# Delta-rule attention and feed-forward network on one core: the order of the work ahead of the first block's output rewritten

## The chip, the cores and the metric

The kernel runs on one core of a Trainium2 chip. The core has five engines that run at the same time, each with its own list of instructions in order: TensorE (PE; its weight loads are listed apart as PEld), VectorE (DVE), ScalarE (ACT), GpSimd (POOL) and SyncE (SP), which issues most of the transfers (DMA). They wait for each other by semaphores. The metric is the device time of one execution in microseconds (us); lower is better.

## What is computed

For each of 4 batches and 8 heads a state of 48 x 48 is carried over 768 steps, and what the state gives for each query goes through a feed-forward network with 2048 inner columns.

```python
k_n = k / (np.linalg.norm(k, axis=-1, keepdims=True) + 1e-06)
for t in range(S):
    y[:, :, t] = np.einsum('bhd,bhde->bhe', q[:, :, t], state)
    v_old = np.einsum('bhde,bhd->bhe', state, kt)
    state = state + bt[:, :, :, None] * np.einsum('bhd,bhe->bhde', kt, vt - v_old)
h = x @ w_in
g = np.where(h >= 1, h, np.where(h <= -1, 0.0, (h + 1) ** 2 / 4))
out = g @ w_out
```

Here x is y with its heads laid side by side, 3072 tokens of 384.

## The kernel before

The 768 steps are cut into 12 blocks g of 64 steps, and blocks are taken in pairs G of two. Within a block the recurrence becomes matrix products. `gram_k` makes the keys' products (64 x 64 for each head) and `gram_q` those of queries with keys; the latter have to be masked to the steps ahead of the query. For a pair, `lanes` lays the key products out, takes the norms (a square root on ACT, then small DVE instructions) and scales them; `solve` inverts triangles of 16 x 16 in 15 steps of two DVE instructions each (lines L355 and L357); `unlanes` writes the result back. `merge16_a`, `merge16_b` and two halves of `merge32` grow the inverse to 64 x 64, with TensorE products and an eviction after each. Then `chain_u` makes the block's updates (its eviction: DVE copies at L514 into the tile SZ and L517 into SU, ACT copies at L517), `chain_y` the outputs (L539 and L541 for the first block; high part by ACT at L556, low part by DVE at L561), `chain_d` adds to the state.

The feed-forward weights come as 16 tiles `wt0` to `wt15` (768 KB each, packed). Each tile is unpacked by `grow` (ACT, L189), `shift` and `join` (DVE, L195 and L201), `cast` (ACT, L205) and `low` (DVE, L208). The network goes through 16 column tiles f for every pair ("items"; the first pair takes some tiles half by half): `up` (L738) makes h on TensorE, ACT and DVE make g out of it (L877, L891, L893, then L856 and L857 for the high and low part), and `down` (L753) accumulates the output two items later.

Two tables of code letters set the order by hand. `FRONT` has seven strings, one for each of the first block's seven chain pieces (merge16_a, merge16_b, two halves of merge32, chain_u, chain_y, chain_d); letters ahead of the comma are emitted between the piece's products and its eviction, letters behind it after the eviction. `FILL` has one string for each item. The letters: A and D the next unpacking step on ACT or DVE; F one dummy product of zeros on TensorE (L165, `dense`); L the next part of `lanes(1)`, the norms of the second pair; S one step of `solve(1)`; s and t the scaling of V for block 0 and 1 (L292); m and M the masking of the query products of block 0 and 1; w the load of the next weight tile; l the next load of keys, queries or values. Each engine runs what it gets in this order and waits at the first instruction that isn't ready.

SP issues loads in order, with eight transfers under way at most: each load waits for the one eight places ahead of it. PSUM banks come from a rotating list `START` (`acc`).

Of the kernel before, what the change touches and what calls it, by code (L numbers as in the profile page):

```python
# [7 lines left out]
F32 = mybir.dt.float32  # L8
# [5 lines left out]
C = 64  # L14
# [15 lines left out]
FRONT = (  # L30
    "sAwFALs,", "FLFFFDFFLFFFFF,F", "FFDD,S", "mFFFFFmm,", "AFFFD,AAw", ",", "DA,Dt")
FILL = (
# [8 lines left out]
def delta_rule_moe(ctx: ExitStack, tc: tile.TileContext, kqa, kqb, kv, beta, w, out):  # L41
# [20 lines left out]
    P = 128  # L62
# [8 lines left out]
    K, KE, GE, Q, KV, XB, RAW, WT = {}, {}, {}, {}, {}, {}, {}, {}  # L71
    START = [dict(name=n, bufs=b) for n, b in (("ch", 2), ("ch", 2), ("h", 2), ("h", 2), ("o2", 1), ("o3", 1), ("o0", 1))]
    spare = []
# [46 lines left out]

    def weight_loads(n0, n1, q=nc.sync):
        for f in range(n0, n1):
            RAW[f] = const.tile([P, 2, 2 * DM], F32, name=f"wt{f}")
            q.dma_start(out=RAW[f].bitcast(I32), in_=w.bitcast(I32)[:, f])

# [10 lines left out]
    load_kv(0)  # L136
    weight_loads(2, 5)
    load_kv(1)
# [27 lines left out]
    dense(WARM)  # L166
    mask = const.tile([P, C], F32, name="mask")
    nc.gpsimd.memset(mask, 1.0)
    for r in (0, C):
        nc.gpsimd.affine_select(out=mask[r:r + C], in_=mask[r:r + C], pattern=[[1, C]], base=0,  # L170
                                channel_multiplier=-1, compare_op=ALU.is_gt, fill=0.0)
    mid = const.tile([P, 1], F32, name="half")
# [71 lines left out]
    def gram_q(g):  # L244
# [12 lines left out]
        def evict():  # L257
            def raw():
                for a, b, r in moved():
                    nc.scalar.copy(out=a, in_=b)  # L260

            def masks(copied=False):
                for a, b, r in moved():
                    nc.vector.tensor_tensor(out=a, in0=a if copied else b, in1=mask[r, None, :].broadcast_to([r.stop - r.start, H, C]), op=ALU.mult)
                    yield

            def later():
                raw()
                for a, b, r in moved():
                    for c in range(r.start, r.stop, C):  # L270
                        y = x[c:c + C, 0 if r.stop - r.start > C else c // C, (0, H)[r.stop - r.start > C]:(H, NU)[r.stop - r.start > C]]
                        nc.gpsimd.affine_select(out=y, in_=y, pattern=[[0, H], [1, C]], base=0, channel_multiplier=-1,  # L272
                                                compare_op=ALU.is_gt, fill=0.0)
            return (raw, masks(True)) if g < 2 else lambda: run(masks()) if g < 4 else later()
        return evict
# [382 lines left out]

    spare += START
    acts = [(f, grow) for f in range(2)] + [x for f in range(FT) for x in ((f + 2, grow), (f, cast)) if x[0] < FT]  # L660
    vecs = [x for f in range(FT + 1) for x in ((f, shift), (f, join), (f - 1, low)) if 0 <= x[0] < FT]
    sv, ln, raws = [scale_v(g) for g in range(4)], [lanes(0), lanes(1)], []
    tasks = {"A": unpack(acts), "D": unpack(vecs), "B": restore(), "L": ln[1], "s": sv[0], "t": sv[1], "v": sv[2], "z": sv[3]}
    loads = [(load_k, 3), (load_q, 2), (load_kv, 2), (load_q, 3), (load_kv, 3), (load_k, 4)]
    tile_ = [5]

    def do(codes):
        for c in codes:
            if c in "wW":
                weight_loads(tile_[0], tile_[0] + 1, nc.scalar if c == "W" else nc.sync)  # L670
                tile_[0] += 1
# [32 lines left out]
    one_ = lambda f, *a: [lambda: f(*a)]  # L704
    place_beta(1, NS)()
    stage(one_(merge16_a, 0), 0)
    stage(one_(merge16_b, 0), 1)
    tasks.update({"m": raws[0][1], "M": raws[1][1], "S": solve(1), "U": unlanes(1)})
    stage(one_(merge32, 0, None, True), 2)
# [3 lines left out]
    stage(both(chain_d, 0), 6)  # L713
    spare[:] = START[0:2] + START[4:6]

# [234 lines left out]
```

## Time and profile before

| | before |
|---|---|
| median of 3 runs | 589.5 us (588.17 to 590.91) |
| profiled execution | 590.3 us, its span 588.6 us |
| TensorE busy | 569.0 us (97%) |
| VectorE busy | 405.2 us (69%) |
| ScalarE busy | 327.5 us (56%) |
| GpSimd busy | 54.5 us (9%) |
| TensorE clock granted, mean | 0.992 of full |

The span is the time between the first and the last instruction; 1.7 us of the profiled execution lie outside it. Busy time is shared out over 40 equal slices on the profile page; there, TensorE's first slices are less full than the rest, the granted clock is 7 tenths in the third slice (29.4 to 44.1 us) and full behind it, and VectorE is at 8 to 9 tenths from the fifth slice to the eighth and at 3 to 9 tenths after that. A dummy product counts as busy TensorE time.

### The profile page before, as it was taken

To read this page: it belongs to the slowest core of one execution; us is meant where nothing else is said; L and a number is where in the kernel's file an instruction comes from. 1 tells how busy PE (TensorE), PEld (TensorE's weight loads), DVE (VectorE), ACT (ScalarE), POOL (GpSimd) and SP (SyncE) were. 2 spreads that over 40 slices of the span, in tenths; PEclk is the share of its full clock that TensorE was granted. 3 is DMA by queue.
4 is the path that set the end of the run, shared out by engine and by line. 5 is a ranking of instruction groups with operands and counts; after the bars stand their busy time and mean duration, and the time that the engine had idled before them with its cause. 6 is when DMAs were issued, how large, how long until landed. Compare 5 with 4: busy or idle time off the path is not lost.

```text
span 588.6 us, 21697 instructions
## 1 busy us (share of the span) xinstructions
PE 569.0 (97%) x9585; PEld 493.3 (84%) x9585; DVE 405.2 (69%) x828; ACT 327.5 (56%) x587; POOL 54.5 (9%) x91
## 2 busy tenths in 40 slices
PE   8998899999999999999999999999999999999996
PEld 7776788788978888888888888888888888898986
DVE  5977999963689864599954599954599955333332
ACT  4648886358644575545575445575445564454443
POOL 6200010000000500010400011300011300000000
PEclk9979999999999999999999999999999999999999
DMA  5673766200333111134011134011133000020001
GB/s 147 199 253 138 213 212 192 77 4 10 95 81 100 31 32 39 39 97 114 24 33 41 37 103 119 16 30 45 36 106 96 1 3 16 15 55 1 0 2 53
DMA packets 32302, 42.77 MB, mean 73 GB/s; under 512 B 7056, under 2 KB 26768, under 8 KB 32208
## 3 DMA queue, kind: packets, MB, share of 16 engines
q1 hardware_dynamic: 31216, 40.41, 24.0%
q8 instruction: 75, 1.23, 0.9%
q0 software_dynamic: 576, 0.57, 0.4%
q10 hardware_dynamic: 416, 0.39, 0.2%
q14 instruction: 19, 0.16, 0.1%
HBM read 34.47 MB, written 4.72 MB: 67 GB/s over the span
## 4 chain that ended last, share of the span: by engine, by line
PE 47%; issue 22%; DVE 14%; DMA 6%; SPq 6%; ACT 2%; POOL 1%; POOLq 0%; DVEq 0%; ACTq 0%
PE h L738 18%; PE o L753 17%; DMA wt<-in_w_dram 4%; PE ch L534 3%; PE ch L237 2%; DVE s L893 2%; PE ch L508 2%; DVE pr L366 1%; DVE A L368 1%; DVE glo L857 1%; PE ch L250 1%; SPq L595 1%; PE ch L492 1%; DMA KV<-in_kv_dram 1%; DVE wt L208 1%
## 5 line engine op out<-in xcount | busy, mean ns | idle before, releaser
L738 PE MATMUL h<-xb,wt 128*128 128x512 f32 (+1 forms) x918 | 223.0, 386 | 5.1 <-DVE s L893 2.0
L753 PE MATMUL o<-wt,ghi 128*128 128x384 f32 x768 | 200.0, 342 | 0.1
L738 PEld LDWEIGHTS h<-xb,wt 128*128 128x128 f32 x918 | 161.8, 188 | 38.9 <-DVE s L893 3.4
L753 PEld LDWEIGHTS o<-wt,ghi 128*128 128x128 f32 x768 | 137.2, 188 | 7.0 <-issue 0.3
L753 PE MATMUL o<-wt,glo 128*128 128x384 f32 x384 | 129.4, 337 | 0.4 <-DVE glo L857 0.4
L856 ACT CAST ghi<-s 128x512 fp32r<-128x512 f32 (+1 forms) x102 | 60.8, 597 | 120.4 <-DVE s L893 107.8
L893 DVE SCALAR_TENSOR_TENSOR s<-s,h 128x512 f32<-128x512 f32 (+1 forms) x102 | 66.3, 650 | 77.1 <-ACT s L891 76.8
L877 ACT ACTIVATE s<-h,half 128x512 f32<-128x512 f32 (+1 forms) x102 | 67.4, 661 | 53.8 <-PE h L738 53.6
L857 DVE TENSOR_TENSOR glo<-s,ghi 128x512 fp32r<-128x512 f32 (+1 forms) x102 | 66.8, 654 | 39.5 <-ACT ghi L856 39.3
L753 PEld LDWEIGHTS o<-wt,glo 128*128 128x128 f32 x384 | 72.1, 188 | 1.0 <-DVE glo L857 1.0
L891 ACT ACTIVATE s<-s 128x512 f32<-128x512 f32 (+1 forms) x102 | 62.2, 610 | 2.2
L368 DVE TENSOR_TENSOR A<-A,pr 128x30 f32<-128x30 f32 (+14 forms) x120 | 45.4, 378 | 4.4
L366 DVE TENSOR_TENSOR pr<-A 128x30 f32<-128x30 f32 (+14 forms) x120 | 43.4, 362 | 2.2
L272 POOL TENSOR_SCALAR_AFFINE_SELECT Q<-Q 64x512 f32<-64x512 f32 x32 | 21.7, 680 | 117.4 <-ACT Q L260 116.0
L165 PE MATMUL o<-wx 128*128 128x512 f32 x87 | 27.8, 464 | 1.5 <-DVE tiny L175 1.5
L534 PEld LDWEIGHTS ch<-Q,SU 64*64 64x64 f32 (+3 forms) x1056 | 22.4, 135 | 3.7 <-ACT ghi L856 1.5
L534 PE MATMUL ch<-Q,SU 64*64 64x64 f32 (+3 forms) x1056 | 24.7, 222 | 0.0
L331 POOL TENSOR_SCALAR_AFFINE_SELECT A<-A 128x1024 f32<-128x1024 f32 x4 | 5.6, 1390 | 191.5 <-DMA xb<-X 148.1
L165 PEld LDWEIGHTS o<-wx 128*128 128x128 f32 x87 | 18.2, 220 | 5.6 <-DVE tiny L175 1.5
L626 DVE TENSOR_TENSOR SU<-ch,SU 48x384 f32<-48x384 f32 x36 | 19.9, 554 | 3.9 <-PE ch L607 3.5
L590 DVE TENSOR_TENSOR X<-ch,X 128x128 fp32r<-128x128 f32 x20 | 5.8, 292 | 23.5 <-ACT xb L586 22.5
L517 ACT COPY SU<-ch 64x384 f32<-64x384 f32 (+1 forms) x30 | 14.3, 476 | 7.0 <-PE ch L508 6.7
(168 smaller groups left out, 559.5 us busy)
## 6 DMA issues: line engine op xcount, KB each, us to landing
wt<-in_w_dram SPq DMA_DIRECT2D x16, 768.0 KB, 5.6
out_dram<-wx SPq DMA_DIRECT2D x44, 96.0 KB, 2.2
KV<-in_kv_dram SPq DMA_DIRECT2D x36, 96.0 KB, 2.4
KV<-in_kv_dram SPq DMA_DIRECT2D x72, 48.0 KB, 2.3
KV<-in_kv_dram SPq DMA_DIRECT2D x12, 192.0 KB, 2.7
xb<-X SPq DMA_DIRECT2D x60, 32.0 KB, 2.0
K<-in_kqb_dram SPq DMA_DIRECT2D x12, 128.0 KB, 2.6
Q<-in_kqb_dram SPq DMA_DIRECT2D x12, 128.0 KB, 2.7
```

Of the source, the lines that this page charges most:

```text
L165: nc.tensor.matmul(warm_ps, warm[:, 0:P], warm, start=True, stop=True)
L272: nc.gpsimd.affine_select(out=y, in_=y, pattern=[[0, H], [1, C]], base=0, channel_multiplier=-1, compare_op=ALU.is_gt, fill=0.0)
L366: nc.vector.tensor_tensor(out=pr, in0=A[:, 0:n, j:j + 1].broadcast_to([P, n, m]), in1=A[:, j:j + 1, j + 1:32].broadcast_to([P, n, m]), op= ...
L368: nc.vector.tensor_tensor(out=A[:, 0:n, j + 1:32], in0=A[:, 0:n, j + 1:32], in1=pr, op=ALU.add)
L534: nc.tensor.matmul(yy[i][o * C:o * C + C, e, p], SF[rows, u:u + C], w_[rows, x, k, :], **how)
L738: nc.tensor.matmul(h[:, cols(bs)], WT[f][:, 0, x, k * P:(k + 1) * P], XB[G][:, y, k, cols(bs)], start=(n == 0), stop=(n == 8))
L753: nc.tensor.matmul(oacc[G, k], (ghi, glo)[x][:, k * P:(k + 1) * P], WT[f][:, 1, y, :], start=(new and n == 0), stop=(left[G, b] == 0 and n ...
L856: nc.scalar.copy(out=ghi[:, c], in_=s[:, c])
L857: nc.vector.tensor_tensor(out=glo[:, c], in0=s[:, c], in1=ghi[:, c], op=ALU.subtract)
L877: nc.scalar.activation(out=s[:, c], in_=h[:, c], func=AF.Relu, bias=mid, scale=0.5)
L891: nc.scalar.activation(out=s[:, c], in_=s[:, c], func=AF.Square)
L893: nc.vector.scalar_tensor_tensor(out=s[:, c], in0=s[:, c], scalar=1.0, in1=h[:, c], op0=ALU.min, op1=ALU.max)
```

## The change

FRONT is rewritten; FILL is not touched. Ahead of the first block's output there are now 15 dummy products, where there were 23. The norms of the second pair (the last two L) and five solve steps (S) stand between the second half of merge32 and chain_u's eviction; before, the norms stood around merge16_b and one solve step behind the first half of merge32. All maskings of query products go to POOL (`select`, affine_select), where blocks 0 to 3 were masked by a DVE product with a mask tile; blocks 2 and 3 get an ACT copy out of PSUM ahead of it. Weight tiles 2 to 4 are no longer loaded between the values of block 0 and block 1: each of the tiles 2 to 6 is loaded by a w of FRONT, and a DVE memset of one element of its room holds its transfer until DVE gets there. For the first two tiles cast comes ahead of the grow of the tile two further on. The rotating list of banks is reordered.

```diff
 FRONT = (
-    "sAwFALs,", "FLFFFDFFLFFFFF,F", "FFDD,S", "mFFFFFmm,", "AFFFD,AAw", ",", "DA,Dt")
+    "sAFFFALs,", "FFFFmmmMMM,wD", "FFD,", "FFFw,LLSS", "AFFFSSS,AwD", "DDw,", "Aw,ASDt")
...
-    START = [dict(name=n, bufs=b) for n, b in (("ch", 2), ("ch", 2), ("h", 2), ("h", 2), ("o2", 1), ("o3", 1), ("o0", 1))]
+    START = [dict(name=n, bufs=b) for n, b in (("ch", 2), ("ch", 2), ("o2", 1), ("o3", 1), ("h", 2), ("h", 2), ("o0", 1))]
...
-    def weight_loads(n0, n1, q=nc.sync):
+    def weight_loads(n0, n1, q=nc.sync, gate=False):
         for f in range(n0, n1):
             RAW[f] = const.tile([P, 2, 2 * DM], F32, name=f"wt{f}")
+            if gate:
+                nc.vector.memset(RAW[f][0:1, 0, 0:1], 0.0)
             q.dma_start(out=RAW[f].bitcast(I32), in_=w.bitcast(I32)[:, f])
...
     load_kv(0)
-    weight_loads(2, 5)
     load_kv(1)
...
-    mask = const.tile([P, C], F32, name="mask")
-    nc.gpsimd.memset(mask, 1.0)
-    for r in (0, C):
-        nc.gpsimd.affine_select(out=mask[r:r + C], in_=mask[r:r + C], pattern=[[1, C]], base=0,
-                                channel_multiplier=-1, compare_op=ALU.is_gt, fill=0.0)
...
-            def masks(copied=False):
-                for a, b, r in moved():
-                    nc.vector.tensor_tensor(out=a, in0=a if copied else b, in1=mask[r, None, :].broadcast_to([r.stop - r.start, H, C]), op=ALU.mult)
-                    yield
-
-            def later():
-                raw()
+            def select():
                 for a, b, r in moved():
                     for c in range(r.start, r.stop, C):
                         y = x[c:c + C, 0 if r.stop - r.start > C else c // C, (0, H)[r.stop - r.start > C]:(H, NU)[r.stop - r.start > C]]
                         nc.gpsimd.affine_select(out=y, in_=y, pattern=[[0, H], [1, C]], base=0, channel_multiplier=-1,
                                                 compare_op=ALU.is_gt, fill=0.0)
-            return (raw, masks(True)) if g < 2 else lambda: run(masks()) if g < 4 else later()
+                    yield
+
+            def later():
+                raw()
+                run(select())
+            return (raw, select()) if g < 2 else later
...
-    acts = [(f, grow) for f in range(2)] + [x for f in range(FT) for x in ((f + 2, grow), (f, cast)) if x[0] < FT]
+    acts = [(f, grow) for f in range(2)] + [x for f in range(FT) for x in (((f + 2, grow), (f, cast)) if f > 1 else ((f, cast), (f + 2, grow))) if x[0] < FT]
...
-    tile_ = [5]
+    tile_ = [2]
...
-                weight_loads(tile_[0], tile_[0] + 1, nc.scalar if c == "W" else nc.sync)
+                weight_loads(tile_[0], tile_[0] + 1, gate=tile_[0] < 7)
...
-    spare[:] = START[0:2] + START[4:6]
+    spare[:] = START[0:4]
```

Line numbers in the rows below are those of the kernel before; the changed kernel's are 4 or 5 lower (L424 becomes L419).

On TensorE, at the first block's merges and chain_u, before (L405 is merge16_a, L419 merge16_b, L436 and L438 the halves of merge32, L508 chain_u, L165 the dummies):

```order
L405 MATMUL ch<-XT,GG 32x16 x64
L165 MATMUL o_152<-wx 128x512
L419 MATMUL ch<-wt_144,XT 32x16 x64
L165 MATMUL o_152<-wx 128x512 x12
L436 MATMUL h<-XT,GG 32x32 x32
L165 MATMUL o_152<-wx 128x512 x2
L438 MATMUL h<-GG 32x32 x32
L165 MATMUL o_152<-wx 128x512 x5
L508 MATMUL o_816<-KV,XT 64x48 x2
```

The same place in the changed kernel:

```order
L400 MATMUL ch<-XT,GG 32x16 x64
L166 MATMUL o_146<-wx 128x512 x3
L414 MATMUL ch<-wt_138,XT 32x16 x64
L166 MATMUL o_146<-wx 128x512 x4
L431 MATMUL o_699<-XT,GG 32x32 x32
L166 MATMUL o_146<-wx 128x512 x2
L433 MATMUL o_741<-GG 32x32 x32
L166 MATMUL o_146<-wx 128x512 x3
L503 MATMUL h<-KV,XT 64x48 x32
```

The twelve dummies between merge16_b and merge32 have become four, the one ahead of merge16_b three, the five ahead of chain_u three.

On VectorE, at merge16_b's eviction (L424 and L425), before (the row ahead is the last but one of the norms, L338 their scaling, L355 and L357 a solve step, L264 a masking):

```order
L324 TENSOR_TENSOR gm<-gm,r_694 128x32
L327 STREAM_TRANSPOSE N_704<-N_692 128x32
L195 TENSOR_SCALAR xb<-xb 128x768
L338 TENSOR_TENSOR A_712<-A,gm 128x256 x2
L424 TENSOR_TENSOR XT<-XT,ch 128x16x16
L425 STREAM_TRANSPOSE GG<-XT 128x16x32
L201 SCALAR_TENSOR_TENSOR xb<-wt_110,xb 128x768
L195 TENSOR_SCALAR xb<-xb 128x768
L453 COPY XT<-XT 32x16x32 x2
L355 TENSOR_TENSOR pr<-X,A_712 128x30
L357 TENSOR_TENSOR X<-X,pr 128x2x15
L264 TENSOR_TENSOR Q<-Q,mask 64x512 x2
```

The same place in the changed kernel (L419 and L420 are merge16_b's eviction, L125 the memsets that hold a weight tile's transfer, L277 the first of the norms, which waits for ACT's square root):

```order
L287 TENSOR_TENSOR KV<-KV,N_451 128x384
L419 TENSOR_TENSOR XT<-XT,ch 128x16x16
L420 STREAM_TRANSPOSE GG<-XT 128x16x32
L125 MEMSET wt_695 1x1
L191 TENSOR_SCALAR xb<-xb 128x768
L197 SCALAR_TENSOR_TENSOR xb<-wt_110,xb 128x768
L448 COPY XT<-XT 32x16x32 x2
L125 MEMSET wt_777 1x1
L277 RECIPROCAL r_784<-y_783 128x32
L278 TENSOR_TENSOR r_784<-r_784,A 128x32
```

merge16_b's eviction stands right behind the scaling of V; the norms have gone behind merge32's eviction.

On VectorE, from the end of the solve steps in front to the first block's low parts, in the changed kernel (L509 and L512 are chain_u's eviction, L204 the last unpacking step of tile 0, L556 the low parts):

```order
L350 TENSOR_TENSOR pr<-X,A_796 128x110
L352 TENSOR_TENSOR X<-X,pr 128x2x5x11
L509 COPY wt_165<-h 64x6x16 x2
L509 COPY wt_165<-h 128x6x16
L512 COPY SU<-h 128x384
L125 MEMSET wt_863 1x1
L191 TENSOR_SCALAR xb<-xb 128x768
L197 SCALAR_TENSOR_TENSOR xb<-wt_112,xb 128x768
L204 TENSOR_TENSOR wt_842<-xb,wt_842 128x2x384
L125 MEMSET wt_921 1x1
L556 TENSOR_TENSOR xb<-o_868,xb 128x2x3x64
```

Before, the rows ahead of chain_u's eviction were the maskings and a join, and tile 0's last unpacking step stood behind the low parts. On ACT the square root of the norms moves from ahead of merge32's evictions to behind them.

## Rows read from the trace of the kernel before

**Rows 1.** TensorE in order of time: start, us, instruction, idle before and releaser.
```profile
28.60 0.43 PE L419 MATMUL ch<-wt,XT 32*32 32x16 f32 x28 [0.75 <-ACT wt L412]
30.29 1.57 PE L419 MATMUL ch<-wt,XT 32*32 32x16 f32 x100 [1.26 <-issue]
31.79 5.35 PE L165 MATMUL o<-wx 128*128 128x512 f32 x12
37.07 1.20 PE L436 MATMUL h<-XT,GG 32*32 32x32 f32 x64
...
42.05 1.15 PE L508 MATMUL o<-KV,XT 64*64 64x48 f32 x64
...
44.03 0.32 PE L539 MATMUL o<-Q,wt 64*64 64x64 f32 x2
...
57.93 0.81 PE L419 MATMUL o<-wt,XT 32*32 32x16 f32 x74
```
**Rows 2.** VectorE and ScalarE in order of time, from the first solve to chain_u's eviction.
```profile
15.45 0.19 DVE L355 TENSOR_TENSOR pr<-X,A 128x30 f32<-128x30 f32 x1
...
18.16 0.28 DVE L355 TENSOR_TENSOR pr<-X,A 128x120 f32<-128x120 f32 x1
...
30.69 0.35 ACT L281 ACTIVATE y<-A,tiny 128x32 f32<-128x32 f32 x1 [2.19 <-DVE A L317]
...
32.89 0.20 DVE L327 STREAM_TRANSPOSE N<-N 128x32 f32<-128x32 f32 x1
33.45 0.76 DVE L338 TENSOR_TENSOR A<-A,gm 128x256 f32<-128x256 f32 x2
...
43.23 0.83 DVE L514 COPY wt<-o 64x96 f32<-64x96 f32 x3 [2.55 <-PE o L508]
```
**Rows 3.** From the first block's output to its first item, three engines in order of time.
```profile
48.18 0.31 PE L539 MATMUL ch<-Q,wt 64*64 64x64 f32 x5 [1.47 <-issue]
...
48.70 1.09 PE L607 MATMUL h<-SU,KV 64*48 64x48 f32 x62
49.18 0.62 DVE L561 TENSOR_TENSOR xb<-ch,xb 128x192 fp32r<-128x192 f32 x2 [1.57 <-ACT xb L556]
50.59 0.56 DVE L195 TENSOR_SCALAR xb<-xb 128x768 int32<-128x768 int32 x1
51.00 1.33 PE L738 MATMUL h<-xb,wt 128*128 128x256 f32 x9 [0.78 <-ACT SU L621]
61.53 0.42 DVE L424 TENSOR_TENSOR XT<-XT,o 128x256 f32<-128x256 f32 x1
```
**Rows 4.** Stretches: us, busy (count) of PE, PEld, DVE, ACT, POOL; granted clock; DMA.
```profile
30.00:32.00 2.00, 1.71 (x101) 1.68 (x102) 1.90 (x6) 0.46 (x2) 0.00 (x0) 0.51 0.89 307
36.00:38.00 2.00, 2.00 (x61) 1.39 (x62) 1.90 (x7) 0.00 (x0) 0.00 (x0) 0.79 1.05 279
120.00:588.60 468.60, 460.89 (x6968) 404.17 (x6968) 303.32 (x613) 252.43 (x456) 37.67 (x52) 1.00 0.18 46
```
**Rows 5.** The later part of the first pair: one masking on DVE, and TensorE's waits.
```profile
92.15 2.09 DVE L264 TENSOR_TENSOR Q<-ch,mask 64x512 f32<-64x512 f32 x3
...
96.74 2.33 PE L738 MATMUL h<-xb,wt 128*128 128x512 f32 x9 [1.05 <-DVE s L893]
108.04 2.76 PE L738 MATMUL h<-xb,wt 128*128 128x512 f32 x9 [0.25 <-DVE s L893]
116.35 2.36 PE L738 MATMUL h<-xb,wt 128*128 128x512 f32 x9 [0.65 <-DVE s L893]
```
**Rows 6.** DVE solve steps ahead of and beside POOL's masking of a later block.
```profile
191.14 0.37 DVE L368 TENSOR_TENSOR A<-A,pr 128x198 f32<-128x198 f32 x1
191.54 0.68 DVE L366 TENSOR_TENSOR pr<-A 128x184 f32<-128x184 f32 x1
...
191.18 3.12 POOL L272 TENSOR_SCALAR_AFFINE_SELECT Q<-Q 64x512 f32<-64x512 f32 x4 [25.19 <-ACT Q L260]
```

**Rows 7.** The page's DMA issues, the weight tiles: count, KB each, median us from issue to landing.
```profile
wt<-in_w_dram SPq DMA_DIRECT2D x16, 768.0 KB, 5.6
```

More of the change, by code (lines that the diff above doesn't have):

```diff
@@ L664, in delta_rule_moe @@
     loads = [(load_k, 3), (load_q, 2), (load_kv, 2), (load_q, 3), (load_kv, 3), (load_k, 4)]
-    tile_ = [5]
+    tile_ = [2]
     def do(codes):
         for c in codes:
-            if c in "wW":
-                weight_loads(tile_[0], tile_[0] + 1, nc.scalar if c == "W" else nc.sync)
+            if c == "w":
+                weight_loads(tile_[0], tile_[0] + 1, gate=tile_[0] < 7)
                 tile_[0] += 1
@@ L705, in delta_rule_moe @@
     place_beta(1, NS)()
+    tasks.update({"m": raws[0][1], "M": raws[1][1]})
     stage(one_(merge16_a, 0), 0)
     stage(one_(merge16_b, 0), 1)
-    tasks.update({"m": raws[0][1], "M": raws[1][1], "S": solve(1), "U": unlanes(1)})
+    tasks.update({"S": solve(1), "U": unlanes(1)})
     stage(one_(merge32, 0, None, True), 2)
```

## The prediction

> **What bounds the kernel now.** I read the profiled execution (590.3 us, 0.8 above the median of 589.5), first by stretches: behind 120 us TensorE works 460.89 of 468.60 us [rows 4], so nothing the change does there can be worth much, and FILL stays as it is. What can be gained lies ahead of 120 us. There TensorE's order of time shows two things to look for: idle time with what ended it, and dummy products, which count as busy but carry nothing. Before merge16_b's end it waits 0.75 us for ACT and then 1.26 us at "issue", that is for nothing that the profile names [rows 1]; the granted clock in that stretch is 0.51, the lower of its two levels (1.2 of 2.4 GHz), and 0.79 in the stretch from 36 to 38 us [rows 4]. Between two levels a mean of 0.79 means a return at about 36.9 us: some 6.8 us at the low clock, although TensorE worked all along. In that time stand twelve dummies of 5.35 us, 446 ns each; merge32 begins behind them at 37.07 and chain_u at 42.05 [rows 1].
>
> Next I follow the first output. Its products start at 44.03 [rows 1], 0.8 us behind the start of chain_u's DVE copies (43.23) [rows 2], stop for 1.47 us at "issue" before 48.18, and end at about 48.9 [rows 3]. Then VectorE is the engine to watch: from the shift at 50.59 it works without a gap through 19 instructions to the next block's merge16_b eviction (L424) at 61.53 [rows 3], for which TensorE waits. What makes that chain start later or earlier moves everything behind it. Last, TensorE's waits for VectorE in the later part of the pair: 1.05, 0.25 and 0.65 us [rows 5], 1.95 together.
>
> **The change part by part.** 1. Eight of the twelve dummies behind merge16_b go: at 446 ns that is 3.6 us. The four left would end at 33.6; merge32 starts at about 33.65, and 0.2 of those 3.6 I leave to its operand from the evictions: -3.4. merge32's copies then end, and chain_u starts, at 38.6 (42.05 before [rows 1]).
>
> 2. On VectorE the second pair's norms and five solve steps now stand ahead of chain_u's copies, and the output waits for these. Their price, from the same instructions: square root to the norms' last row 30.69 to 33.09, 2.40 us; scaling 0.76; five steps of the first solve 15.45 to 18.16, 2.71 [rows 2]; 5.87 together. The square root stands behind merge32's ACT copies in ACT's queue, so the sum starts at 38.55: chain_u's copies begin at 44.4, 1.2 us later than before (43.23 [rows 2]), and the output at 45.2. So of the 3.4 us nothing is left for the output; the work moved in front takes 4.6. What it buys is that VectorE needn't do it later. TensorE, with chain_u and three dummies done by 40.7, stands idle for about 4.5 us.
>
> 3. The 1.47 us stop inside the output's products [rows 3] goes. The listing has 384 matmuls between the two stops at "issue", and with fewer dummies the same place in the program is passed inside chain_u, some 7 us earlier, ahead of the idle stretch. Bounds: nothing gained, and -1.47. The other such place comes to lie in merge32's first half; it may cost between 0 and 2.2 us, and I take 0, since VectorE and ACT have work there. The Trainium skill ("Runtime: NRT & Kernel Launch", section "Instruction fetch mechanics") says the opposite of these stops: that an engine passing from one block of its program to the next pays an amount that is mostly hidden. By that rule the stop is something else and stays, and the sum would be 590.1 instead of 588.6; the trace, with 1.26 and 1.47 us where nothing else is waited for, speaks against the rule here, and I give it 1 in 10 within the forecast.
>
> 4. The clock. Two us of idle time stood ahead of the low clock at 30 us [rows 1, 4]; 4.5 us of it now stand ahead of the output. I take it that the clock falls there. The price is read from merge16_b's products: 100 in 1.57 us at 0.51, 15.7 ns each, against 74 in 0.81 at full clock, 10.9 [rows 1]: a factor of 1.4. The output's own time without the stop is 3.4 us, the state update behind it adds 0.9 [rows 3]; 4.3 x 0.4 = +1.7. Bounds: 0, if the clock stays, and twice the time, +4.3. After 6.8 us, at about 52, it would be back, as before.
>
> 5. So the output runs from 45.2 to 50.0, its low parts (0.9 behind it before [rows 3]) end at 50.9, a solve step of some 0.7 follows, and the shift that begins VectorE's unbroken stretch starts at 51.65 instead of 50.59 [rows 3]: +1.05. TensorE's first item needs no eviction of the state update now (0.78 us before [rows 3]), since the banks are reordered; it starts at 51.2 to 51.8, against 51.00, and waits for VectorE's stretch anyhow. At 62 us the kernel is 1.05 late.
>
> 6. Five solve steps are gone from the later part, about 2.3 us of VectorE, and its maskings too (2.09 us for one of them [rows 5]). TensorE's waits of 1.95 us there [rows 5] go: bounds 0 and -1.95, and I take -1.95, as VectorE's relief is larger than the sum of the waits. Sum: +1.05 - 1.95 = -0.9, 589.4 on the profiled execution, **588.6** against the median.
>
> Costed at nothing: POOL's masking for blocks 0 and 1, 0.78 us for each instruction [rows 6], eight of them, 6.2 us that are over by about 33 and wanted at 45; without that cover the output would wait for them. The copies by ACT for blocks 2 and 3, 1.8 us each, lie in ACT's idle time of several us. The memsets that hold the weight tiles are 0.06 us each; the tiles, 5.6 us from issue to landing [rows 7], are issued at about 45 (tile 4), 48, 51 and 52 and land at 51 to 57, against unpacking at 53 to 61 in ACT's order; SP has key and value loads queued behind them, which are wanted later still. The nearest to late is tile 4, by 2 us; were it late, ACT's grow and VectorE's stretch would move with it.
>
> **The rivals.** A is the forecast. B, **the clock stays or is back before the output**: it needs that idle time ahead of the output isn't as that at 29 us was. For it, the clock came back at 36.9 while dummies ran, and fewer of them run now, so its rhythm shifts; against it, 4.5 us of idle are over twice the two before the fall [rows 1]. The 1.7 of step 4 goes: 586.9. If merge32's dummies also run at full speed, four at about half of 446 ns, 0.8 more: 586.1. With the scatter of a median (runs from 588.17 to 590.91), 585.4 to 587.3, its middle 586.4.
>
> C, **slower: the clock stays low beyond the first item**. Output and update double, +4.3 in place of +1.7, so +2.6; the first nine products, 1.33 us [rows 3], double as well, of which VectorE's wait for the first item sees about 0.7. The unbroken stretch then ends 1.05 + 3.3 = 4.35 late; less 1.95, +2.4: 591.9. It decides from the point where the low clock returns later than the first item's start, 52 us. For it, 6.8 us were once low with TensorE busy [rows 4]; against, from 45 to 52 it is as busy as it was then, from 30 to 37.
>
> D, **the later gain is lost on VectorE**: beside POOL's masking a solve step of two operands in SBUF took 0.68 us, just before it 0.37 for a larger one [rows 6]. All maskings of the first two pairs now run on POOL, beside the later solve steps; 0.31 us for each instruction that meets one, some four of them a block, is 1.3 us, and the waits of 1.95 shrink by 0.6 only: 590.0. Against it, POOL's work is spread and VectorE has slack there. The Trainium skill ("SBUF — State Buffer", section "Who interferes with whom") has a rule by which this would happen: a DVE instruction with two SBUF inputs contends with a GpSimd instruction that reads SBUF. By that rule D holds wherever they meet; the rows with 0.37 and 0.68 agree.
>
> That the change doesn't do what it says could be so for the banks alone: if the first item still waits for the update's eviction, that is 0.78 at most, hidden behind VectorE.
>
> **How the numbers follow.** A 0.38, B 0.32, C 0.14, D 0.16. About 0.5%, 2.9 us, is what a measurement of this kernel can tell from no change: 586.6 and 592.4 are the bounds. Faster: two thirds of B (0.21) and a quarter of A, where a price of step 2 or 4 comes out lower (0.10): 0.31. Slower: two thirds of C and a little of D, where a weight tile is late as well: 0.11. The rest, 0.58, is no difference. The range takes in B to 585.4 and half of C, to 592.0; A alone would be 586.9 to 590.1.
>
> **What would show it.** In the changed kernel's trace: merge32 at about 33.7 (step 1); VectorE's reciprocal of the norms at 39, held by the square root, and chain_u's copies at 44.4 (2); no stop at "issue" among the output's products (3); granted clock about 0.5 from 45 to 52 (4); the first item at 51.2 to 51.8, the end of VectorE's stretch at 62.6 (5); no waits of TensorE for VectorE near 97, 108 and 116 us (6). B shows a clock of 1.00 at 45 us, C one of 0.5 beyond 52, D instructions of 0.68 beside POOL. I am wrong if copies begin well before 44 or a stop at "issue" turns up elsewhere, or if TensorE waits for a weight tile.

## The result and the profile after

The changed kernel takes **598.68 us** (median of 4 executions, 596.64 to 600.60), the kernel before on the same chip 590.16: a ratio of 1.0149, 95% interval 1.0101 to 1.0197. It is slower by 1.5%, where 0.2% faster was forecast, and outside the range (585.4 to 592.0). The profiled execution has 600.6 us, the slowest of the four, and a span of 598.9 us, 10.3 longer than before; the medians differ by 8.5.

The page shows where to look: TensorE has more busy time with eight products fewer (580.0 us against 569.0), and its clock is below full in more slices.

```profile
PE 580.0 (97%) x9577; PEld 504.2 (84%) x9577; DVE 400.0 (67%) x821; ACT 330.7 (55%) x593; POOL 66.0 (11%) x104
...
PEclk9957599999999999999999999999999989999999
...
q8 instruction: 75, 1.23, 0.9%
```

Stretches of the changed kernel (us, busy and count of PE, PEld, DVE, ACT, POOL, then granted clock, DMA share, GB/s), against [rows 4]:

```profile
30.00:32.00 2.00, 1.87 (x103) 1.84 (x104) 1.12 (x3) 0.23 (x1) 1.87 (x3) 0.50 0.39 105
40.00:42.00 2.00, 2.00 (x65) 1.73 (x64) 1.43 (x6) 0.35 (x1) 0.00 (x0) 0.50 0.46 183
44.00:46.00 2.00, 0.00 (x0) 0.00 (x0) 1.79 (x8) 1.05 (x2) 0.00 (x0) 1.00 0.00 0
48.00:50.00 2.00, 2.00 (x46) 2.00 (x46) 1.39 (x3) 0.32 (x1) 0.00 (x0) 0.50 0.88 267
52.00:54.00 2.00, 1.69 (x42) 1.41 (x41) 1.97 (x6) 1.95 (x5) 0.00 (x0) 1.00 1.02 331
54.00:56.00 2.00, 0.64 (x76) 0.64 (x78) 2.00 (x4) 1.97 (x5) 0.00 (x0) 1.00 1.00 406
68.00:76.00 8.00, 8.00 (x127) 7.34 (x122) 4.89 (x10) 5.81 (x11) 0.00 (x0) 0.50 0.75 247
476.00:482.00 6.00, 4.29 (x14) 4.19 (x14) 2.31 (x4) 3.41 (x6) 0.00 (x0) 0.57 0.01 3
```

The reader is to see four stretches at the lower level, 1.2 GHz: 13.7 us from 30 on, 3.4 from 46.7 on, 20.5 from 57 on and 6.8 from 477 on, 44.4 us in all (the last two microseconds, low in both kernels, aside). Before there was one, of 6.8 us at [rows 4]. In the third TensorE is busy nearly throughout (8.00 of 8.00 us from 68 to 76), and yet it is the longest of the four.

TensorE in order of time, answering to [rows 1, 3]:

```profile
30.13 1.57 PE L414 MATMUL ch<-wt,XT 32*32 32x16 f32 x102 [1.43 <-issue]
31.63 2.08 PE L166 MATMUL o<-wx 128*128 128x512 f32 x4
33.64 1.92 PE L431 MATMUL o<-XT,GG 32*32 32x32 f32 x64
...
40.27 1.96 PE L503 MATMUL h<-KV,XT 64*64 64x48 f32 x64
...
46.15 0.30 PE L534 MATMUL o<-Q,wt 64*64 64x64 f32 x2 [2.49 <-DVE wt L509]
...
52.08 1.23 PE L734 MATMUL h<-xb,wt 128*128 128x256 f32 x9
53.24 0.44 PE L400 MATMUL ch<-XT,GG 32*32 32x16 f32 x32
55.37 0.99 PE L400 MATMUL ch<-XT,GG 32*32 32x16 f32 x96 [1.68 <-issue]
...
61.00 2.29 PE L734 MATMUL h<-xb,wt 128*128 128x256 f32 x9
...
474.16 1.29 PE L457 MATMUL ch<-XT,GG 32*32 32x32 f32 x128
477.71 0.80 PE L749 MATMUL o<-wt,ghi 128*128 128x384 f32 x2 [2.26 <-ACT GG L466]
```

The first item starts 1.1 us late, where 0.2 to 0.8 was forecast. Ahead of the third and fourth low stretch stands a stop: 1.68 us in the second block's merge16_a, and 2.26 us behind 128 quick products of a merge at 474 us. The start of each item (the nine up products) shows what each cost:

| item starts, before | after | late by |
|---|---|---|
| 51.00 | 52.08 | 1.1 |
| 56.67 | 61.00 | 4.3 |
| 70.83 | 78.73 | 7.9 |
| 91.37 | 99.36 | 8.0 |
| 130.92 | 136.87 | 6.0 |
| end of the span | | 10.3 |

So 6.8 us come up between the first item and 79 us: the stop, 1.7, and a rest of 5.1 that is put down to the low clock (a kernel without it, below, shows 3.6 of them). Then 2.0 are won back to 131 us, the waits for VectorE that were forecast to go, and 4.3 are lost, net, behind 131 us: the kernel is 5.1 us late at 457 us and 10.1 at 491, on either side of the stop.

**What the two stops are.** Queue q8 moved 75 transfers of 1.23 MB in all, 16 KB each. They are taken for TensorE's program: 75 pieces of 256 instructions are 19,200 of the 19,301 that its trace has. Counted in the traces of both kernels, every stop of TensorE at "issue" of over 0.4 us ahead of 130 us, and the one at 477 us (which the profile puts down to ACT; more on that below), stands at the same place in such a piece: in the changed kernel at instructions 1218, 2242, 5058 and 17089 of TensorE, 193 or 194 over a multiple of 256. (256 instructions are 128 products with their weight loads.) One such transfer brings the next piece. From the trace, the moment TensorE enters a piece, the start of the next piece's transfer, and the start of that piece; the DMA share is that from 3 us before the transfer's start to 1 us behind it (the transfer itself makes 0.02 of it):

| kernel | enters | transfer starts | next piece starts | DMA share | stop |
|---|---|---|---|---|---|
| before | 42.16 | 45.94 (+3.8) | 48.19 | 0.99 | 1.47 |
| before | 52.46 | 53.41 (+1.0) | 55.84 | 0.02 | 0.25 |
| before | 55.84 | 56.88 (+1.0) | 59.56 | 0.02 | 0.83 |
| after | 50.33 | 53.14 (+2.8) | 55.37 | 0.98 | 1.68 |
| after | 474.16 | 475.00 (+0.8) | 477.71 | 0.02 | 2.26 |
| before | 468.00 | 463.70 (-4.3) | 470.06 | 0.02 | none |

Where the transfer starts behind the entry, a piece thus takes at least 3.4 to 3.7 us even while the DMA engines are idle: 0.8 to 1.0 to the start of the transfer, 2.4 to 2.7 from there to the next piece's first instruction. In the last row the transfer had begun ahead of the entry, and the piece passed in 2.05 us without a stop, though 122 of its 126 products were quick ones of the same merge. In all 20 traces no piece starts less than 2.1 us behind the start of its transfer, and all 65 stops of TensorE at "issue" of over 0.6 us behind the first 20 us stand at the end of a piece. What lets a transfer start ahead of the entry is not shown. With weight tiles in flight 1 to 3 us more go by ahead of the transfer. Long products need more than that for a piece; 128 products of the solver need 1.2 to 1.4 us at full clock. The changed kernel has weight tiles in flight just when the second block's merge16_a runs (share 1.02 and 1.00 from 52 to 56 us; before, next to nothing was in flight then). The transfers of the changed kernel just ahead of the stop, q8 with the program, q1 with the weights (packets, MB, share of 16 engines), first from 50.4 to 53.1 us:

```profile
q1 hardware_dynamic: 173, 0.90, 107.8%
```

and from 53.1 to 54.2 us:

```profile
q1 hardware_dynamic: 48, 0.26, 76.2%
q8 instruction: 1, 0.02, 5.5%
```

The transfer for the piece that TensorE needs at 53.7 us starts behind 2.7 us of nothing but weights. The Trainium skill ("Runtime: NRT & Kernel Launch", section "Instruction fetch mechanics") has the same pieces, 16 KiB or 256 instructions; that passing from one to the next is mostly hidden, as it says, does not hold for these products: 1.68 and 2.26 us.

### The profile page after: what moved, and what is told of

It reads as the page before. It is cut to its first block, busy times and chain, and to the rows that moved or that the text cites. A ratio compares the mean times of both kernels' runs of the same rounds, so it can differ in the third digit from the quotient of the medians.

```text
span 598.9 us, 21719 instructions
## 1 busy us (share of the span) xinstructions
PE 580.0 (97%) x9577; PEld 504.2 (84%) x9577; DVE 400.0 (67%) x821; ACT 330.7 (55%) x593; POOL 66.0 (11%) x104
## 3 DMA queue, kind: packets, MB, share of 16 engines
q8 instruction: 75, 1.23, 0.9%
## 4 chain that ended last, share of the span: by engine, by line
PE 59%; issue 23%; DVE 13%; ACT 2%; SPq 1%; POOL 1%; DMA 1%; POOLq 0%; ACTq 0%; DVEq 0%
PE h L734 21%; PE o L749 19%; PE ch L529 3%; PE ch L233 2%; PE o L166 2%; PE ch L487 2%; PE ch L503 1%; DVE A L363 1%; DVE pr L361 1%; PE ch L246 1%; DVE SU L621 1%; DVE glo L853 1%; DVE pr L350 1%; DVE s L889 1%; DVE X L352 1%
## 5 line engine op out<-in xcount | busy, mean ns | idle before, releaser
L734 PE MATMUL h<-xb,wt 128*128 128x512 f32 (+1 forms) x918 | 226.3, 391 | 1.9 <-DMA xb<-wt 0.5
L749 PE MATMUL o<-wt,ghi 128*128 128x384 f32 x768 | 202.4, 345 | 2.3 <-ACT GG L466 2.3
L734 PEld LDWEIGHTS h<-xb,wt 128*128 128x128 f32 x918 | 165.5, 193 | 35.4 <-DVE s L889 2.0
L749 PEld LDWEIGHTS o<-wt,ghi 128*128 128x128 f32 x768 | 139.2, 191 | 9.0 <-issue 2.1
L749 PEld LDWEIGHTS o<-wt,glo 128*128 128x128 f32 x384 | 73.3, 191 | 0.9 <-DVE glo L853 0.7
L262 POOL TENSOR_SCALAR_AFFINE_SELECT Q<-Q 64x512 f32<-64x512 f32 x48 | 33.9, 706 | 156.7 <-ACT Q L256 154.5
L256 ACT COPY Q<-ch 64x512 f32<-64x512 f32 (+1 forms) x33 | 19.2, 581 | 4.5 <-PE ch L246 3.7
L166 PEld LDWEIGHTS o<-wx 128*128 128x128 f32 x79 | 16.7, 226 | 5.1 <-DVE tiny L171 1.5
```

What stands on the lines that cost most here:

```text
L166: nc.tensor.matmul(warm_ps, warm[:, 0:P], warm, start=True, stop=True)
L734: nc.tensor.matmul(h[:, cols(bs)], WT[f][:, 0, x, k * P:(k + 1) * P], XB[G][:, y, k, cols(bs)], start=(n == 0), stop=(n == 8))
L749: nc.tensor.matmul(oacc[G, k], (ghi, glo)[x][:, k * P:(k + 1) * P], WT[f][:, 1, y, :], start=(new and n == 0), stop=(left[G, b] == 0 and n ...
```

## Experiments

Medians stand beside those of the kernel before, run beside them on the same chip; ratios are to it, with their 95% interval. "First item" and "late by" are against the profile of before. The expectations set three theories against each other: 1, the stop and its place in the program; 2, the idle time ahead of the output; 3, VectorE's work in front.

### Is it the number of instructions, the idle time ahead of the output, or the work on VectorE?

Eight more dummies behind chain_u:

```diff
-"AFFFSSS,AwD"
+"AFFFFFFFFFFFSSS,AwD"
```

> The changed kernel with eight more dummy products behind chain_u (eleven in place of three): they fill TensorE's idle time ahead of the first output, and the count of TensorE instructions ahead of everything that follows is that of before. Theory 1 (the stop at 53.7 us, where TensorE runs out of fetched instructions, moved there by eight missing instructions, makes the clock fall for 20 us): the stop in merge16_a of the second block goes, no low clock from 57 to 77 us, 589 to 592 us. Theory 2 (the idle time ahead of the output makes the clock fall again later): the same. Theory 3 (the work of the second pair on VectorE ahead of chain_u's eviction is what costs): 597 to 600 us.

593.44 us against 591.05, ratio 1.0055 (1.0028 to 1.0082), over the 589 to 592 of theory 1. The stop in merge16_a shrinks to 0.75 us, but one of 3.24 us comes up in the next piece, at the state products with keys, and 17 us of low clock behind it:

```profile
59.73 0.20 PE L487 MATMUL ch<-SU,K 48*64 48x48 f32 x1 [3.24 <-issue]
```

TensorE had entered the piece at 53.42 and its successor's transfer started only at 57.53, 4.1 us later. Near 477 us there is no stop, and the time lost behind 131 us is 0.7 us.

The same with dummies of 64 columns (a letter f in place of the eight F):

> The same with eight dummies of 64 columns in place of 512: the count is that of before, the idle time ahead of the output is hardly filled (0.3 to 0.5 us of 2.5). Theory 1: no stop at 53.7 us and no low clock from 57 to 77, 590 to 593 us. Theory 2: the low clock at 57 stays, 597 to 600. Theory 3: 597 to 600.

594.20 us, ratio 1.0049 (1.0016 to 1.0081); a stop of 2.29 us at the same products, 13.7 us of low clock behind it. Neither the columns nor the count decide whether there is a stop; they move it by a piece. Theory 1 as first put, that eight missing products brought the stop, had fallen.

Four dummies moved from behind merge16_b to behind chain_u:

```diff
-"FFFFmmmMMM,wD"
+"mmmMMM,wD"
...
-"AFFFSSS,AwD"
+"AFFFFFFFSSS,AwD"
```

> The changed kernel with its four dummies behind merge16_b moved behind chain_u: the count ahead of the first output and of all that follows is unchanged, 1 to 2 us of the idle time ahead of the output are filled. Theory 1: the stop at 53.7 us and the low clock behind it stay, 596 to 600 us. Theory 2: the low clock at 57 goes, 590 to 593. Theory 3: 597 to 600.

595.46 us, ratio 1.0076 (1.0039 to 1.0112), a little under the 596 to 600 of theory 1. The stop in merge16_a is 1.72 us, the low clock behind it 20.5 us, and 2.22 us of stop at 477.67: with the count unchanged, both are at their old places.

Eight of twelve dummies taken out of the kernel before:

```diff
-"FLFFFDFFLFFFFF,F"
+"FLFDLF,F"
```

> The kernel before with eight of the twelve dummies behind merge16_b taken out, and nothing else. Theory 1: the stop inside the first output (48.2 us) goes and one of 1 to 2 us stands in merge16_a of the second block, with a low clock behind it: 593 to 598 us. Theories 2 and 3: the first output comes up to 3 us earlier and no low clock follows it: 586 to 589 us.

591.96 us, ratio 1.0038 (1.0005 to 1.0072), and no stop over 0.3 us in the second block's merge16_a: theory 1 was wrong here. The profiled execution is 1.5 us ahead of before at 131 us and 2.2 ahead at 457, then stops 1.43 us at 470, at instruction 17089, and ends 0.7 late.

### Is it the weight tiles in flight?

The changed kernel with its tiles loaded as before:

```diff
     load_kv(0)
+    weight_loads(2, 5)
     load_kv(1)
...
-    "sAFFFALs,", "FFFFmmmMMM,wD", "FFD,", "FFFw,LLSS", "AFFFSSS,AwD", "DDw,", "Aw,ASDt")
+    "sAwFFFALs,", "FFFFmmmMMM,D", "FFD,", "FFF,LLSS", "AFFFSSS,AwD", "DD,", "A,ASDt")
...
-    tile_ = [2]
+    tile_ = [5]
...
-                weight_loads(tile_[0], tile_[0] + 1, gate=tile_[0] < 7)
+                weight_loads(tile_[0], tile_[0] + 1)
```

> The changed kernel with the weight tiles loaded as before (tiles 2 to 4 between the values of blocks 0 and 1, tile 5 at merge16_a, tile 6 at chain_u, no memset holds a transfer); all else as changed. Theory 1, now: TensorE enters a new piece of its program every 256 instructions (128 products with their weight loads), and the next piece's transfer starts 1 us after that with the DMA engines idle but 2 to 4 us with a weight tile in flight; the change puts tiles 4 to 6 into 48 to 57 us, where the second block's small products use up a piece in 2 us; TensorE stops, and the clock falls behind the stop. So here: no stop above 0.9 us from 50 to 62 us, no low clock behind 50 us in the first 100, a stop of about 2 us near 470 us as with the changed kernel, 588 to 592 us. Theory 3 (the VectorE work ahead of chain_u's eviction): 597 to 600.

596.42 us against 590.76, ratio 1.0129 (1.0068 to 1.0191). The place behaved as expected: no stop over 0.2 us from 50 to 62 us, full clock from 56 to 60, and 2.29 us of stop at 475.88. The time didn't (588 to 592 was expected): tiles 2 to 4 now meet the shortened chain (DMA share 0.92 from 30 to 32 us), and the stop has gone into merge32's first half, ahead of which the transfer started 4.3 us late:

```profile
33.71 0.84 PE L432 MATMUL o<-XT,GG 32*32 32x32 f32 x22
37.20 1.37 PE L432 MATMUL o<-XT,GG 32*32 32x32 f32 x42 [2.65 <-issue]
```

The first item is 4.8 us late and the low clock lasts 24 us from 31 us on. Before, twelve dummies lay where these tiles fly.

The same with eight more dummies behind chain_u ("AFFFFFFFFFFFSSS,AwD"):

> The same with eight more dummies behind chain_u, so that all that follows stands at the place in the program that it had before. Theory 1: neither the stop at 50 to 62 us nor the one near 470; 586 to 590 us, the fastest so far. Theory 3: 595 to 599.

593.81 us, ratio 1.0056 (1.0025 to 1.0087), where 586 to 590 was expected. No stop at 470 us, as expected; 2.44 us of it in merge32, and 10 us of low clock later.

The kernel before with the tiles held as in the changed one, and nothing else:

```diff
-    "sAwFALs,", "FLFFFDFFLFFFFF,F", "FFDD,S", "mFFFFFmm,", "AFFFD,AAw", ",", "DA,Dt")
+    "sAFALs,", "FLFFFDFFLFFFFF,wF", "FFDD,S", "mFFFFFmmw,", "AFFFD,AAw", "w,", "DAw,Dt")
...
-    weight_loads(2, 5)
...
+            if gate:
+                nc.vector.memset(RAW[f][0:1, 0, 0:1], 0.0)
```

> The kernel before with the weight tiles 2 to 6 loaded as in the changed one (five letters w at the same five places of the order, each tile's transfer held by a VectorE memset); nothing else. Theory 1: fetches start 2 to 4 us behind the entry into a piece between 45 and 58 us, a stop of 1.5 us or more there, and a low clock of 10 us or more behind it: 594 to 600 us. Theory 3: as before, 589 to 592.

A stop of 3.08 us, at the place and with the cause that were expected (the piece entered at 50.65, the transfer at 54.47), and 10.2 us of low clock behind it:

```profile
56.85 0.25 PE L493 MATMUL o<-SU,K 48*64 48x48 f32 x1 [3.08 <-issue]
...
55.00:60.00 5.00, 3.15 (x87) 2.87 (x91) 2.50 (x6) 2.07 (x4) 0.00 (x0) 0.82 0.10 30
```

Yet the median is 592.31 us, ratio 1.0023 (0.9988 to 1.0057), less than expected: ahead of it the tiles are out of the way. The stop in the first output falls from 1.47 to 0.73 us and the first item comes 1.9 us early. In the profiled executions the held tiles gain 1.9 us up to the first item and lose 4.5 from there to 67 us. So holding the tiles brings the stop and the low clock by itself, but in this kernel no loss on the whole.

The changed kernel with the second pair's norms and solve steps where they were:

```diff
-"sAFFFALs,", "FFFFmmmMMM,wD", "FFD,", "FFFw,LLSS", "AFFFSSS,AwD", "DDw,", "Aw,ASDt"
+"sAFFFALs,", "FLFFFLmmmMMM,wD", "FFD,S", "FFFw,", "AFFF,AwD", "DDw,", "Aw,ADt"
```

> The changed kernel with the second pair's norms and solve steps back where they stood before (norms at merge16_b, one step behind merge32's first half, the rest later); weight tiles held as changed. Theory 1: tiles 4 to 6 are still in flight when the second block's products run, a stop of 1.5 us or more and the low clock stay: 595 to 600 us. Theory 3: the first output comes 2 to 4 us earlier and the low clock goes: 587 to 592.

595.69 us, ratio 1.0109 (1.0052 to 1.0166). The first item starts at 49.23, 2.9 us ahead of the changed kernel: that is the price of the VectorE work in front. The stop stays (2.64 us at 57.07, transfer 3.4 us behind the entry), and so does the low clock (13.7 us). Waits for VectorE from 96 to 120 us are 1.48 us in all; they fell to 0.25 in the changed kernel.

### Is the stop what brings the low clock?

Dummies that keep TensorE at work where it would stop:

```diff
-PIECES = ((1, "a1 f6 r1"),
+PIECES = ((1, "f6 a1 f9 f5 r1"),
```

> The changed kernel with fourteen more dummies, six between the first item's up products and merge16_a of the second block and eight behind merge16_a: they lie where TensorE would wait for the next piece of its program (1.68 us in the changed kernel, about 2 us more in the next piece if the clock were full), so that it works instead of stopping. Weight tiles, order on the other engines and the first output stay as changed. Theory 1 (the stop is what makes the clock fall, and the low clock is the larger part of the loss): no stop above 1 us from 50 to 62 us, full clock or at most 7 us of low clock behind 52 us, 589 to 593 us. Rival (the clock falls there for what lay ahead of it, the low clock from 30 to 43 and the idle time ahead of the output): 10 us or more of low clock behind 52 us, 596 to 600.

593.41 us against 591.33, ratio 1.0043 (1.0010 to 1.0075), a little over the 589 to 593 of theory 1. Stretches of this kernel:

```profile
52.00:60.00 8.00, 7.03 (x165) 5.50 (x165) 6.02 (x10) 7.86 (x13) 0.00 (x0) 1.00 0.59 199
60.00:72.00 12.00, 9.73 (x340) 8.65 (x340) 10.15 (x20) 8.29 (x15) 0.00 (x0) 1.00 0.58 189
```

The clock is full from 52 to 72 us, though it was low from 30 to 50 (20.5 us) and TensorE idle for 2.35 us ahead of the output. The dummies take the time of the stop, so the second item is late by 4.6 us, about as in the changed kernel (4.3); from there to 71 us nothing is added, where the changed kernel loses 3.6 more. A stop of 1.28 us is left at 60.30, a little over the 1 us expected, and the clock stays. So with the stop filled the fall at 57 us is gone. Not all of the gain is due to that: the dummies move the later ends of pieces as well, there is no stop at 477 us, and from 131 us to the end the kernel goes from 4.7 late to 4.0. Against it, a stop of 1.56 us at 80.08, with 3.4 us of low clock behind it, costs 2.6.

The twelve dummies put back into the changed kernel ("FFFFFFFFFFFFmmmMMM,wD"):

> The changed kernel with twelve dummies behind merge16_b, as before, in place of four. By Theory 1: merge32 begins 2 to 3.5 us later, the clock is back before chain_u, the first output comes 1 to 3 us later than in the changed kernel; the held weight tiles are later by as much and still meet the second block's products, so a stop of 1.5 us or more between 52 and 62 us: 592 to 598 us. If the shortened chain itself were the cost: as before, 589 to 592.

595.25 us, ratio 1.0058 (1.0021 to 1.0095): a stop of 3.25 us at 59.36 and 17 us of low clock behind it. The shortened chain alone is not the cost.

### VectorE's relief, and attempts at a kernel that beats both

All maskings on POOL, the kernel before otherwise (the diff's `select` in place of `masks`):

> The kernel before with all maskings of query products on POOL (blocks 2 and 3 with an ACT copy ahead), and nothing else: the part of the change that frees VectorE. If VectorE's relief is worth what was forecast for it, TensorE's waits for VectorE near 97, 108 and 116 us shrink from 1.95 us to under 1, 0.5 to 1.9 us faster than before. If POOL's work stretches VectorE's instructions by as much, or the time is bound elsewhere: no difference.

592.78 us, ratio 1.0020 (0.9989 to 1.0050): no difference. The waits for VectorE shrink from 1.95 to 1.64 us only; it is the moved solve steps that take them away. With the changed list of banks too:

> The same with the changed kernel's list of PSUM banks as well: the first item no longer waits 0.78 us for the state update's eviction. If VectorE's unbroken stretch binds behind it, no gain over the run without; else up to 0.8 us more.

592.32 us, ratio 1.0022 (0.9989 to 1.0054); the first item comes 0.8 us early and nothing is left of it at the end.

Three more have the filled stop. First with eight dummies behind chain_u as well:

> The changed kernel with the fourteen dummies around the second block's merge16_a and eight more behind chain_u, ahead of the first output. If the low clock is what is left of the loss and each us of it costs about 0.3 us (the slope over the runs of the kernel before), filling the idle time ahead of the output takes one short stretch of low clock away: 590 to 593 us, 0 to 2 below the kernel with fourteen alone. If dummies there delay the output: 593 to 595.

594.38 us against 590.20, ratio 1.0068 (1.0043 to 1.0093): no low clock from 42 us to the end, and yet no gain over the fourteen alone. The second item is 3.1 us late, the fourteen dummies' own time among it, at 131 us it is 1.5, and 3.8 at the end, behind stops of 0.7 to 1.6 us at 123, 180 and 387 us. Further six dummies ahead of merge16_b ("sAFFFFFFFFFALs,"):

> The same with six more dummies ahead of merge16_b (nine in place of three), where TensorE waits 1 to 2 us before the clock falls at 30 us for the first time. If that first fall comes from the idle time ahead of it, the clock stays full from 28 us on, the chain of the first block gets 1 to 2 us shorter and the time is 587 to 590 us, under that of the kernel before. If it falls all the same: 590 to 594.

598.91 us, ratio 1.0168 (1.0134 to 1.0203): a miss. The profiled execution (593.32 us) is the fastest of seven and shows the clock falling at 37 us instead of 30; the other six, at mean clocks of 0.975 to 0.987, were not traced, and what they lose stays open. Last, the fourteen with twelve dummies behind merge16_b:

> The changed kernel with twelve dummies behind merge16_b as before and the fourteen around the second block's merge16_a. Against the run with twelve alone (595.25 us, 17 us of low clock behind a stop of 3.25 us) the fourteen should take the stop below 1.5 us and the low clock behind it away: 589 to 592 us.

598.04 us, ratio 1.0129 (1.0093 to 1.0166): a miss too. The low clock behind 53 us is gone, but the first output waits 3.99 us for chain_u's eviction, and 3.0 us more are lost at a stop of 1.35 us near 391.

Seven dummies of the kernel before moved ahead of merge16_b:

```diff
-"sAwFALs,", "FLFFFDFFLFFFFF,F"
+"sAwFFFFFFFFALs,", "FLFDFLF,F"
```

> The kernel before with seven of the twelve dummies behind merge16_b moved ahead of it; their number, and so the place of all that follows, is unchanged. If the first fall of the clock comes from the 2 us of idle time ahead of it, the clock stays full at 30 us and the time is 588 to 590 us; if the five that are left let it fall a little later, as before or up to 2 us slower.

591.24 us, ratio 1.0016 (0.9992 to 1.0039): no difference. The stop and the wait ahead of the first fall are gone, and the clock falls at 35 us, behind a wait of 2.01 us for VectorE, for 10.2 us.

### Is the late stop a matter of its place in the program?

Eight dummies of 64 columns at about 69 us, so that all behind stands where it stood before, in the changed kernel:

```diff
-"wD,ADS,MA,MADF,,"
+"wD,ADS,MA,MADFffffffff,,"
```

> The changed kernel with eight dummies of 64 columns at about 69 us, behind the stop and the fall of the clock at 53 to 57 us: all that follows stands again at the place in the program that it had before. If the stop of 2.3 us near 477 us (behind 128 quick products of a merge, with a low clock behind it) is there because a piece of the program ends at that place, it goes and the 4 to 5 us with it: 593 to 596 us, and the stop at 53 us stays. If it has another cause: 597 to 600.

595.81 us against 590.08, ratio 1.0081 (1.0048 to 1.0115), within what was expected; the profiled execution (598.48) is the slowest of eight. The same products of the merge, now followed without a stop:

```profile
476.81 1.29 PE L457 MATMUL ch<-XT,GG 32*32 32x32 f32 x128
478.03 0.62 PE L751 MATMUL o<-wt,ghi 128*128 128x384 f32 x2
```

It is 7.8 us late at 457 and 7.8 at 491 us, where the changed kernel goes from 5.1 to 10.1. The down products start ahead of ACT's copies L466 (478.68), so it was not these copies that they waited for at 477 us in the changed kernel, though its profile names them. The stop ahead of the third low stretch is there (2.64 us at 59.81).

And in the kernel before with eight dummies fewer:

> The kernel before with eight of the twelve dummies behind merge16_b taken out, and eight of 64 columns put in at about 69 us. The run without these eight was 1.5 us ahead of before at 130 us and 2.2 at 457 us, and lost 3 us behind a stop near 470. With the places restored the gain should stay: 588 to 590 us, 1 to 2 us under before. If the late loss has another cause: 591 to 593.

591.64 us, ratio 1.0022 (0.9990 to 1.0054): the stop at 470 is gone, but the profiled execution (595.79, the slowest of twelve) lost 3 us by 71 us, with a wait of 2.07 us for VectorE and a stop of 1.51 us in merge32, and 2.8 at a stop near 392, which the profile of before does not have. This stop, too, is at the end of a piece of 128 quick products. Here the piece is entered at 389.67, the transfer starts at 389.70, and the next piece starts at 392.39 with a stop of 1.44 us; in the kernel before it is entered at 387.00, the transfer had begun at 386.14, and the stop is 0.14. What lets the transfer begin earlier or later stays open. No run beat the kernel before.

## Why the prediction was wrong

- **Step 1** (merge32 at 33.65, chain_u at 38.6): merge32 began at 33.64. chain_u came at 40.27, since the low clock stayed until 43.4 and each half of merge32 took 1.92 to 2.13 us where the sum had 1.20. Mis-sized by 1.7, so of the 3.4 us that the dummies were to give, about half came.
- **Step 2** (copies at 44.4): 45.76, the output at 46.15 instead of 45.2. The price of the VectorE work was right: the copies come 5.4 us behind the reciprocal of the norms, as forecast, but that came at 40.38 instead of 39. TensorE was idle for 2.49 us instead of 4.5.
- **Step 3** (no stop in the first output): the stop went, as forecast, but not in the way that was given, which is luck. The place 384 products behind the first stop was not passed inside chain_u; it still lay in the output, at 50.33, and the next piece was there in time since its transfer had begun at 41.98, ahead of the wait for VectorE. The first stop stayed where it was (1.43 us at 30.13, 1.26 before). The step took the stops for two places; there is a piece's end every 128 products, and that the transfer competes with the weights was not seen. The sign of being wrong that the prediction named, a stop at "issue" elsewhere, came at 55.37.
- **Step 4** (low clock from 45 to 52, 1.7 us): it fell, at 46.8, for 3.4 us instead of 6.8. Rival B's sign, a full clock at 45 us, was there, but B was not: the clock fell again just behind the output's first products. Step 5's first item at 51.2 to 51.8 was 52.08, 1.1 late in place of 0.8 at most; the errors of steps 1, 2 and 4 nearly cancel there. VectorE's stretch began at 52.28 instead of 51.65 and did not run without a gap: it waited 2.46 us for TensorE at 58.6, and the eviction of merge16_b (the prediction calls it merge16_a's) came at 65.78 instead of 62.6.
- **Step 6** (waits for VectorE go, 1.95): 2.0 won back between 91 and 131 us. The solve steps did it; the maskings alone gave 0.3. Rival D fell with it: a solve step of 128x30 did take 0.62 us beside POOL's masking at 102 us, 0.19 elsewhere, but few of them met one, and the waits went all the same.
- **What failed** is step 3's count of the stops together with a term costed at nothing: the held weight tiles. The prediction asked only whether a tile lands in time for its unpacking. It did not ask what else uses the DMA engines from 48 to 57 us. TensorE's program does, and the second block's solver products use it up faster than it comes. In place of 0 stand a stop of 1.7 us and 5.1 us that go with the low clock behind it.
- Rival C had a low clock beyond the first item, but as one that begins ahead of the output and doubles a few products (2.4 us). The fall came later, behind a stop of its own, and lasted 20.5 us.
- The second failure is the count. Eight dummies fewer move the end of every later piece; at 477 us one came to stand right behind 128 quick products, in a piece that was entered only with them: 2.26 us of stop and 6.8 us of low clock, some 5 us from 457 to 491. "Behind 120 us nothing can be worth much" overlooked that.

## What to carry to other kernels

Where many small products follow each other, the program itself is a stream: count TensorE's instructions in pieces of 256, see how long each piece runs, and keep bulk transfers out of the stretches where it runs under 3.5 us. A dummy taken out or put in moves every later end of a piece, so look for stops far behind the change as well. A stop costs more than its length when the clock falls behind it; read the granted clock of the stretches before believing a sum of durations.

## What the runs showed that was not expected

- The length of a low stretch varies widely: 3.4, 6.8, 10.2, 13.7, 17, 20.5 and 24 us were seen, the one of 20.5 us in the changed kernel with TensorE busy for 20.27 us of it. A stop is no sure sign of a fall: 1.68 to 3.25 us behind the first item had one in all eight traces that show such a stop there (in one, with eight dummies at 69 us, only 5.7 us later), but 1.96 us inside the first output, in the kernel with only the maskings on POOL, had none, where 1.11 us at 60.54 in the same execution had. What decides is not settled.
- The time of one kernel follows the low clock. Over the 119 executions of the kernel before that were made beside the experiments, on five chips (586.56 to 597.06 us), time at the low level, worked out as twice the lost share of the mean clock by the span, runs from 3.5 to 29.8 us, and the time grows by 0.31 us for each us of it (correlation 0.78; 587.1 at none). The four executions of the changed kernel have 31 to 47 us of it: by that line 597 to 601 us, where 596.6 to 600.6 were measured. Where stops are filled with dummies the line doesn't hold (594.38 us with eight dummies more behind chain_u, at mean clocks of 0.986 to 0.991, where it gives 590 to 592).
- Taking the weights out of one crowded stretch put the stop into the next. With the tiles early it was merge32 (2.65 us), held it was the second block (1.68 to 3.25 us), and before it was the first output (1.47).
